# Hash attention and a SwiGLU block on one core: sums stored in two pieces, and x brought earlier, in the second block

## Chip, cores and metric

One core of one Trainium2 chip runs the whole program. The metric is the device time of an execution in microseconds (us). A kernel's time is the median of several executions.

## The reference

Attention with a hash mask, then a gated feed-forward block on its output:

```python
# q, k, v: (4, 8, 768, 64)   proj: (64, 6)
q_bucket = sum((q @ proj > 0) * 2**i);  k_bucket = sum((k @ proj > 0) * 2**i)
scores = where(q_bucket[:, None] == k_bucket[None, :], q @ k.T / 8, -1e9)
x = softmax(scores) @ v                  # all heads side by side: x is (3072, 512)
g = x @ w_gate                           # (512, 1536)
out = (g * sigmoid(g) * (x @ w_val)) @ w_out     # w_out: (1536, 512), out: (3072, 512)
```

## The kernel before

The program first does the attention (to 314 us of the span), and beside it and beside the first block splits the weights; then the feed-forward block in three blocks of 1024 rows of x. The stretch of this change is the second block and the start of the last one.

**Three parts for each number.** The matrix engine is fed with a rounded part, a rest and a difference of the two, in float32 form. So every operand is three arrays, made by three operations: `high` (ACT rounds), `low` (DVE takes the rest) and `diff` (DVE subtracts). Weights are split once and kept in DRAM tiles (`ram`); a ring of six tiles in on-chip memory is filled from there by `bring()`, whose loads GpSimd (POOL) issues in order.

**First and second block.** For each f of 12 there is a U: `one` (products of high and low, PE, tile `a`) for gate and value, then `other` (products of diff, tile `n`). ACT copies `a` into `n` (L849) before `other` may add to it, applies Silu (L862) for the gate, DVE multiplies (L872), and ACT and DVE split the result into `hid` (L881, L892, L895). A U is four steps, its slots 0 to 3; it takes 10.9 us of PE. After f = 3, 6, 9 and 11 there is a D, which multiplies three hids with `w_out`: eight chunks (slots 0 to 7), each with two ACT operations (L967, L923) and one of DVE (L973). So the order is U0 to U3, D 0, U4 to U6, D 1, U7 to U9, D 2, U10, U11, D 3.

**The last block** replaces 8 products of quarter matrices by 7, of sums of quarters of the weights and of x. Its sums are made in the second block, beside its products: for each p of 6 a gate and a value sum of weights (`("w", p, side)`), and four sums of x (`("x", j, side)`: xa, xb, ya, yb). `add` (L1090 to L1113, DVE) makes the sum in a tile `made`, of which there are two, one for each side (tags x2 and x3); `high` (L1119, ACT), `low` (L1125, L1127, DVE) and `diff` (L1134, L1138, DVE) split it; then the tile is stored to DRAM (`sums` and `xsums`, L1136 and L1140), by a DMA that SP issues. The next sum of the same side waits until that store has left the tile. The plan of slots is written out by hand with `put`: a step put at ("U", 4, 2) is recorded behind slot 2 of U4. Each engine runs its instructions in the order in which they were recorded, and each waits by semaphores for what it needs; SP's DMAs, too, are issued in the recorded order.

**What is brought for the last block.** x as the attention left it (`load_x`, L1050) goes into three tiles `words`; from its first quarter `first_quarter` makes B11 (L1199, L1203, L1207) into the tile x2, that a `made` had. `bring_sum` (L1188) loads the sums of x: T1 into x3, T2 and T3 into x0 and x1 when the second block's x has been used up; `fourth_sum` (L1216) loads T4 into the three `words` tiles.

**A group of the last block** is seven products, A11 to A22, one for each of the slots 1 to 6 that stand between them. Behind each, ACT and DVE take the result out (L1354, L1357, L1360) and free its bank. What remains of the group before, above all the split of its hid (`high`, `low`, `diff`: L1418, L1421, L1426), is recorded with `then(k, ...)` and runs at slot k of the next group.

Of the kernel before, what the change touches and what calls it, by code (L numbers as in the profile page):

```python
# [8 lines left out]
FP32 = mybir.dt.float32  # L9
# [10 lines left out]
def kernel(  # L20
# [771 lines left out]
    def gated_block(scope):  # L792
# [253 lines left out]
        def load_x(block, prs):  # L1046
            for pr in prs:
                t = wordp.tile([P, PIECE, 2], I32, tag="words", name="words")
                x = t.rearrange("p f w -> p (f w)").bitcast(FP32)
                nc.sync.dma_start(x, kept_x[pr][:, block * WB - S : (block + 1) * WB - S])  # L1050
                raw_x[block, pr] = x
# [70 lines left out]
        def low(key):  # L1122
            t = made[key]
            if key[0] == "w":
                tt(r32(t[:, :, 1]), t[:, :, 1], t[:, :, 0], op=ALU.subtract)  # L1125
            else:
                nc.vector.scalar_tensor_tensor(out=r32(t[:, :, 1]), in0=t[:, :, 0], scalar=-STEP,  # L1127
                                               in1=t[:, :, 1], op0=ALU.mult, op1=ALU.add)

        def diff(key):  # L1130
            t = made.pop(key)
            kind, n, side = key
            if kind == "w":
                nc.vector.scalar_tensor_tensor(out=r32(t[:, :, 2]), in0=t[:, :, 1], scalar=-STEP,  # L1134
                                               in1=t[:, :, 0], op0=ALU.mult, op1=ALU.add)
                nc.sync.dma_start(sums["gv"[side], n], t)  # L1136
            else:
                tt(r32(t[:, :, 2]), t[:, :, 0], t[:, :, 1], op=ALU.subtract)  # L1138
                for e in range(2):
                    nc.sync.dma_start(xsums[2 * side + e][:, n], t[:, e])  # L1140


        plan = {}
# [1 line left out]
        def put(kind, f, at, op, *args):  # L1145
            plan.setdefault((kind, f, at), []).append(lambda: op(*args))
# [23 lines left out]
                    put(*here, op, key)  # L1170
        put("U", 2, 0, load_x, LAST, (0, NP // 2))
        put("U", 4, 2, load_x, LAST, (1, 1 + NP // 2))
        xa, xb, ya, yb = (("x", j, side) for j in range(2) for side in range(2))
        for kind, f, at, op, key in (("U", 4, 0, add, xa), ("U", 4, 1, add, xb),
                                     ("U", 4, 2, high, xa), ("U", 5, 0, high, xb),
                                     ("U", 4, 3, low, xa), ("U", 4, 3, diff, xa),
                                     ("U", 5, 1, low, xb), ("U", 5, 1, diff, xb),
                                     ("D", 1, 3, add, ya), ("D", 1, 5, add, yb),
                                     ("D", 1, 5, high, ya), ("D", 1, 7, high, yb),
                                     ("D", 1, 6, low, ya), ("D", 1, 7, diff, ya),  # L1180
                                     ("U", 7, 0, low, yb), ("U", 7, 0, diff, yb)):
            put(kind, f, at, op, key)

# [2 lines left out]
        def bring_sum(i, pool, tag):  # L1186
            t = pool.tile([P, 2, 3, PIECE], FP32, tag=tag, name="xparts")
            nc.sync.dma_start(t, xsums[i])  # L1188
            xs[f"T{i + 1}"] = lambda v, j: t[:, j, v]

        def first_quarter():

            t = xparts_p.tile([P, 2, 3, PIECE], FP32, tag="x2", name="xparts")
            xs["B11"] = lambda v, j: t[:, j, v]
            x = [raw_x.pop((LAST, j))[:, 0:PIECE] for j in range(2)]

            def high():
                for j in range(2):
                    nc.scalar.activation(r32(t[:, j, 0]), x[j], AF.Copy, scale=TOWARD / STEP)  # L1199

            def low():
                for j in range(2):
                    nc.vector.scalar_tensor_tensor(out=r32(t[:, j, 1]), in0=t[:, j, 0], scalar=-STEP,  # L1203
                                                   in1=x[j], op0=ALU.mult, op1=ALU.add)

            def diff():
                nc.vector.tensor_tensor(r32(t[:, :, 2]), t[:, :, 0], t[:, :, 1], op=ALU.subtract)  # L1207

            return [high, low, diff]

        def fourth_sum():
            ts = []
            for v in range(3):
                t = wordp.tile([P, PIECE, 2], I32, tag="words", name="words")
                t = t.rearrange("p f w -> p (f w)").bitcast(FP32).rearrange("p (j c) -> p j c", j=2)
                nc.sync.dma_start(t, xsums[3][:, :, v])  # L1216
                ts.append(t)
            xs["T4"] = lambda v, j: ts[v][:, j]

        gens = {}  # L1220

# [6 lines left out]
        for i, (kind, n) in enumerate(order):  # L1228
            b, f = divmod(n, NF if kind == "U" else NF // NQ)
            if b == LAST - 1:  # L1230
                if kind == "U" and f == NF - 2:
                    assert not made
                    load_x(LAST, range(NP // 2))
                    splits.extend(first_quarter())
                elif kind == "U" and f == NF - 1:
                    bring_sum(0, xparts_p, "x3")
                    load_x(LAST, range(NP // 2, NP))
            elif (kind, f) == ("D", NF // NQ - 2):
                load_x(b + 1, range(NP // 2))
            elif kind == "U" and f >= NF - 2:  # L1240
                assert len(added) == NPIECE
                splits.extend(split_x(b + 1, f - NF + 2))
                if f == NF - 1:
                    load_x(b + 1, range(NP // 2, NP))
            if kind == "U":
                if b == LAST - 1 and f % 2 and f < NF - 1:
                    for side, what in enumerate("gv"):
                        ahead_of[what].append(lambda side=side: add(("w", f // 2, side), n))
            for at, atom in enumerate(gens.pop(i, None) or atoms_of(kind, n)):
                if kind == "U" and at == 2:  # L1250
                    sow_next(i)
                tail = atom()
                for entry in list(tails):
                    entry[0] -= 1
                    if not entry[0]:
                        tails.remove(entry)
                        entry[1]()
                if tail:
                    tails.append([1 if n % NF == NF - 1 else 2, tail])
                if kind == "U" and f >= NF - 2 and at and splits:  # L1260
                    splits.pop(0)()
                if kind == "D" and f == NF // NQ - 1:
                    if at == 0:
                        more = [split_x(b + 1, pr) for pr in range(NP // 2, NP)]
                        if b == LAST - 1:
                            for i_ in (1, 2):
                                bring_sum(i_, xparts_p, f"x{i_ - 1}")
                    if b == LAST - 1:
                        if at in (1, 2, 5, 7, 8, 9):
                            more[at in (2, 7, 9)].pop(0)()  # L1270
                        if at == 7:
                            fourth_sum()
                    elif at in (0, 7, 10):
                        for x in more:
                            x.pop(0)()
                count[0] += 1
                if left and count[0] in (4, 6, 11):
                    left.append(left.pop(0)())
                    left[:] = [f for f in left if f]
                    if count[0] == 4:  # L1280
                        bring(2)
                if kind == "U":
                    pace = (1, 2, 2, 2)
                elif n == 0:
                    pace = (0, 0, 0, 2, 1, 2, 2, 2)
                else:
                    pace = (0, 0, 1, 0) + (1,) * 8
                if b == LAST - 1:
                    for op in plan.pop((kind, f, at), ()):
                        op()  # L1290
                    continue
                if b == LAST - 2 and (kind, f) == ("D", NF // NQ - 1):
                    for op, key in opening.get(at, ()):
                        op(key)
                for _ in range(pace[at]):
                    step = next(mine, None)
                    if step:
                        step()
# [24 lines left out]
        def group(what, p):  # L1323
# [124 lines left out]
            then(2, lambda: low(0))  # L1448
            then(3, lambda: diff(0))
            then(3, lambda: high(1))  # L1450
            then(4, lambda: low(1))
            then(6, lambda: diff(1))

        gates = {}
# [48 lines left out]
```

## Time and profile before

| what | value |
|---|---|
| runs, us | 908.23, 905.15, 907.61 (median 907.61) |
| profiled execution, us | 906.43 |
| its span, us | 904.5 |
| PE busy | 892.4 us, 99% |
| DVE, ACT, POOL busy | 75%, 59%, 12% |
| second block | 510.8 to 717.4 us of the span |
| last block | from 717.4 us |

Times within the profile are counted from the start of the span; 1.9 us of the execution lie outside it. PE is matmul, ACT ScalarE, DVE VectorE, POOL GpSimd, SPq the sequencer of SyncE, which issues DMAs. A row of the timeline gives the start, the time to the end of the last instruction in it, the engine, the line of the kernel, the operation, what it writes and reads, and in brackets the idle time before it and who ended that. An idle engine that nobody waits for costs nothing.

### The profile page before, as it was taken

How to read it: one execution, taken by the hardware profiler on the slowest of the kernel's cores; microseconds unless marked ns; L12 is line 12 of the kernel's file. 1: busy time of each engine (PE TensorE's matmuls, PEld its weight loads, DVE VectorE, ACT ScalarE, POOL GpSimd, SP SyncE). 2: the span in 40 equal slices, each digit the busy share in tenths (PEclk: the TensorE clock that was granted, in tenths of full speed). 3: DMA queues.
4: the chain of work that ended last, by engine and by line, in shares of the span. 5: the costliest groups of instructions: out<-in, count | busy, mean ns of one | idle time of the engine just before them, and what ended most of it. 6: DMA issues, size and time to landing. Idle time of an engine off the chain costs nothing.

```text
span 904.5 us, 12799 instructions
## 1 busy us (share of the span) xinstructions
PE 892.4 (99%) x4731; PEld 624.3 (69%) x4731; DVE 678.8 (75%) x877; ACT 533.7 (59%) x782; POOL 107.0 (12%) x211
## 2 busy tenths in 40 slices
PE   9999999999999999999999999999998999999998
PEld 5444444444444488888888788867886877888887
DVE  6779999999988956649484978588682668377386
ACT  6788988788888645541423245355453667376470
POOL 2001100010001210101010010100010122121110
PEclk9999999999999999999999999999999999999999
DMA  7667778877787699776757787788869998297482
GB/s 180 111 147 183 188 205 193 211 214 217 226 196 214 218 355 355 265 268 213 278 192 278 287 324 299 297 303 327 312 235 377 374 355 284 102 331 265 158 278 93
DMA packets 149980, 224.06 MB, mean 248 GB/s; under 512 B 104000, under 2 KB 113696, under 8 KB 148000
## 3 DMA queue, kind: packets, MB, share of 16 engines
q0 software_dynamic: 25312, 128.99, 40.6%
q1 hardware_dynamic: 123200, 93.08, 34.3%
q10 hardware_dynamic: 1408, 1.20, 0.6%
q8 instruction: 37, 0.61, 0.3%
q14 instruction: 23, 0.19, 0.1%
HBM read 157.81 MB, written 64.59 MB: 246 GB/s over the span
## 4 chain that ended last, share of the span: by engine, by line
PE 74%; DVE 11%; issue 8%; DMA 5%; ACT 2%; POOL 1%; SPq 0%; POOLq 0%; DVEq 0%; ACTq 0%
PE sc L605 17%; PE av L636 14%; PE a L806 14%; PE o L806 13%; PE n L806 6%; PE y L806 3%; DMA sums_ram<-made 2%; PE joint L677 1%; DMA ring<-sums_ram 1%; DVE o L973 1%; PE joint L497 1%; PE x L806 1%; DVE hid L1421 1%; DVE hid L892 1%; DVE made L1125 1%
## 5 line engine op out<-in xcount | busy, mean ns | idle before, releaser
L806 PE MATMUL o<-ring,hid 128*128 128x512 f32 (+1 forms) x872 | 200.6, 389 | 2.3 <-DVE hid L892 1.0
L806 PEld LDWEIGHTS o<-ring,hid 128*128 128x128 f32 x872 | 162.4, 188 | 39.2 <-ACT o L923 2.1
L806 PE MATMUL a<-xparts,ring 128*128 128x512 f32 x768 | 178.1, 389 | 0.0
L806 PEld LDWEIGHTS a<-xparts,ring 128*128 128x128 f32 x768 | 144.1, 188 | 30.5 <-issue 0.6
L615 ACT ACTIVATE A<-sc 128x768 f32<-128x768 f32 x192 | 154.0, 814 | 1.6 <-PE sc L605 0.8
L605 PE MATMUL sc<-qT,kT 64*128 64x384 f32 x768 | 153.0, 483 | 0.0
L636 PE MATMUL av<-A,vraw 128*64 128x386 f32 (+1 forms) x768 | 127.7, 488 | 0.0
L849 ACT ACTIVATE n<-a 128x1024 f32<-128x1024 f32 x46 | 46.4, 1009 | 136.2 <-PE a L806 129.1
L308 POOL DMA_DIRECT2D ring<-ram x108 | 60.6, 563 | 389.7 <-PE n L806 119.1
L636 PEld LDWEIGHTS av<-A,vraw 128*64 128x64 f32 x768 | 53.7, 136 | 73.3 <-issue 62.4
L806 PE MATMUL n<-xparts,ring 128*128 128x512 f32 x384 | 93.3, 395 | 4.4 <-ACT n L849 4.4
L605 PEld LDWEIGHTS sc<-qT,kT 64*128 64x128 f32 x768 | 68.8, 187 | 39.8 <-issue 35.1
L806 PEld LDWEIGHTS n<-xparts,ring 128*128 128x128 f32 x384 | 72.9, 191 | 21.0 <-ACT n L849 5.8
L973 DVE TENSOR_TENSOR o<-o 128x512 f32<-128x512 f32 x84 | 56.9, 686 | 35.5 <-ACT o L967 20.1
L892 DVE SCALAR_TENSOR_TENSOR hid<-hid,v 128x1024 fp32r<-128x1024 f32 (+1 forms) x26 | 29.7, 1141 | 47.5 <-ACT hid L881 47.5
L967 ACT ACTIVATE o<-o 128x512 f32<-128x512 f32 x56 | 33.3, 596 | 53.5 <-PE o L806 52.5
L605 PE MATMUL sc<-qb,kb 64*128 64x384 bf16 x384 | 63.5, 323 | 0.0
L659 DVE SCALAR_TENSOR_TENSOR both<-A 128x1536 f32<-128x1536 f32 x32 | 55.5, 1733 | 3.9 <-ACT A L615 2.3
L663 DVE TENSOR_TENSOR both<-both,A 128x1536 f32<-128x1536 f32 x32 | 56.0, 1749 | 1.7
L806 PE MATMUL y<-xparts,ring 128*128 128x512 f32 x216 | 55.0, 390 | 0.0
L806 PEld LDWEIGHTS y<-xparts,ring 128*128 128x128 f32 x216 | 40.5, 188 | 8.9 <-DMA ring<-ram 0.5
L605 PEld LDWEIGHTS <-kb 64*128 64x128 bf16 x384 | 19.6, 94 | 32.5 <-issue 9.0
(219 smaller groups left out, 1074.8 us busy)
## 6 DMA issues: line engine op xcount, KB each, us to landing
ring<-ram POOLq DMA_DIRECT2D x96, 768.0 KB, 6.6
sums_ram<-made SPq DMA_DIRECT2D x12, 1536.0 KB
ring<-sums_ram POOLq DMA_DIRECT2D x24, 768.0 KB, 6.5
ram<-stage POOLq DMA_DIRECT2D x22, 768.0 KB, 4.3
ram<-stage SPq DMA_DIRECT2D x14, 768.0 KB
vraw<-in_v_dram SPq DMA_DIRECT2D x16, 384.0 KB
words<-xram SPq DMA_DIRECT2D x12, 512.0 KB
xsums<-made SPq DMA_DIRECT2D x8, 768.0 KB
```

The source lines that it names most:

```text
L308: nc.gpsimd.dma_start(t.bitcast(FP32)[:, :, cols], src[:, :, cols])
L497: nc.tensor.matmul(tile_[i * BLOCK : (i + 1) * BLOCK, 0:HQ], hash_w, T[name, n][:, half * HQ : (half + 1) * HQ], start=True, stop=True)
L605: nc.tensor.matmul(banks_of[u][:, h], x["k", n][rows, ks], x["q", n][rows, qs], start=start, stop=stop)
L615: nc.scalar.activation(weights(u)[:, :, 0:HQ], banks_of.pop(u), AF.Exp, scale=SCALE * (1.0 if units[u][0] else OFF / 2))
L636: nc.tensor.matmul(ps[h * D : (h + 1) * D, 0:width], raws["v", n][:, h, c, :], a[:, h, 0:width], start=c == 0, stop=c == NCH - 1)
L659: nc.vector.scalar_tensor_tensor(out=t, in0=first, scalar=S * EPS / P / 2, in1=now, op0=ALU.add, op1=ALU.add)
L663: nc.vector.tensor_tensor(t, t, now, op=ALU.add)
L806: nc.tensor.matmul(ps, w, x, start=start, stop=stop, **more)
L849: nc.scalar.activation(n_, a, AF.Copy, scale=-(STEP + 1))
L892: nc.vector.scalar_tensor_tensor(out=l_, in0=h_.bitcast(FP32), scalar=-STEP, in1=v_, op0=ALU.mult, op1=ALU.add)
L967: nc.scalar.activation(accs[c], t[:, 0], AF.Copy, scale=STEP + 1)
L973: nc.vector.tensor_tensor(accs[c], accs[c], t[:, 1], op=ALU.subtract)
```

## The change

Four edits. The sums are stored in two pieces: high and low right after `low`, and the difference after `diff`. x for the last block is loaded earlier: the first two of its four pieces are put at U8 and the third at U9 (before: U10, U11), the fourth stays at U11; the steps of `first_quarter` are put one slot later each than they ran, and its `bring_sum` at U10. T4 comes in three loads, put at slots 0, 5 and 7 of D 3, instead of all three at slot 7. The order of the operations for ya and yb in D 1 is another: ya's rounding is put one slot earlier, and ya's `low` ahead of yb's `add`. In the last block the `low` of the second hid runs at slot 6 instead of 4.

```diff
+            keep(key, slice(0, 2))          # at the end of low(key)
+
+        def keep(key, parts):
+            kind, n, side = key
+            t = made[key]
+            if kind == "w":
+                nc.sync.dma_start(sums["gv"[side], n][:, :, parts], t[:, :, parts])
+                return
+            for e in range(2):
+                nc.sync.dma_start(xsums[2 * side + e][:, n, parts], t[:, e, parts])
 
         def diff(key):
...
-                nc.sync.dma_start(sums["gv"[side], n], t)
...
-                for e in range(2):
-                    nc.sync.dma_start(xsums[2 * side + e][:, n], t[:, e])
+            keep(key, slice(2, 3))
+            made.pop(key)
...
+        put("U", 8, 0, load_x, LAST, range(NP // 2))
+        put("U", 9, 0, load_x, LAST, (NP // 2,))
...
-                                     ("D", 1, 3, add, ya), ("D", 1, 5, add, yb),
-                                     ("D", 1, 5, high, ya), ("D", 1, 7, high, yb),
-                                     ("D", 1, 6, low, ya), ("D", 1, 7, diff, ya),
+                                     ("D", 1, 3, add, ya), ("D", 1, 4, high, ya),
+                                     ("D", 1, 5, low, ya), ("D", 1, 5, add, yb),
+                                     ("D", 1, 6, diff, ya), ("D", 1, 7, high, yb),
                                      ("U", 7, 0, low, yb), ("U", 7, 0, diff, yb)):
...
+        fourth = []
+
         def fourth_sum():
-            for v in range(3):
-                ...
+            t = wordp.tile([P, PIECE, 2], I32, tag="words", name="words")
...
+            nc.sync.dma_start(t, xsums[3][:, :, len(fourth)])
+            fourth.append(t)
...
                 if kind == "U" and f == NF - 2:
-                    load_x(LAST, range(NP // 2))
-                    splits.extend(first_quarter())
-                elif kind == "U" and f == NF - 1:
-                    bring_sum(0, xparts_p, "x3")
-                    load_x(LAST, range(NP // 2, NP))
+                    steps = first_quarter()
+                    put("U", f, 1, bring_sum, 0, xparts_p, "x3")
+                    put("U", f, 2, steps[0])
+                    put("U", f, 3, steps[1])
+                    put("U", f + 1, 0, steps[2])
+                    put("U", f + 1, 0, load_x, LAST, (NP - 1,))
...
-                        if at == 7:
+                        if at in (0, 5, 7):
                             fourth_sum()
...
-            then(4, lambda: low(1))
+            then(6, lambda: low(1))
```

More of the change, by code (lines that the diff above doesn't have):

```diff
@@ L1128, in low @@
                                                in1=t[:, :, 1], op0=ALU.mult, op1=ALU.add)
+            keep(key, slice(0, 2))
[7 more added lines that the diff above has]
+                nc.sync.dma_start(xsums[2 * side + e][:, n, parts], t[:, e, parts])
         def diff(key):
-            t = made.pop(key)
-            kind, n, side = key
-            if kind == "w":
+            t = made[key]
+            if key[0] == "w":
                 nc.vector.scalar_tensor_tensor(out=r32(t[:, :, 2]), in0=t[:, :, 1], scalar=-STEP,
                                                in1=t[:, :, 0], op0=ALU.mult, op1=ALU.add)
-                nc.sync.dma_start(sums["gv"[side], n], t)
             else:
                 tt(r32(t[:, :, 2]), t[:, :, 0], t[:, :, 1], op=ALU.subtract)
-                for e in range(2):
-                    nc.sync.dma_start(xsums[2 * side + e][:, n], t[:, e])
+            keep(key, slice(2, 3))
+            made.pop(key)
         plan = {}
@@ L1209, in first_quarter @@
             return [high, low, diff]
+        fourth = []
         def fourth_sum():
-            ts = []
-            for v in range(3):
[L1214 to L1218, printed above, removed]
+            t = wordp.tile([P, PIECE, 2], I32, tag="words", name="words")
+            t = t.rearrange("p f w -> p (f w)").bitcast(FP32).rearrange("p (j c) -> p j c", j=2)
+            nc.sync.dma_start(t, xsums[3][:, :, len(fourth)])
+            fourth.append(t)
+        xs["T4"] = lambda v, j: fourth[v][:, j]
         gens = {}
```

## The prediction

> **What bounds the kernel now.** I read the page first: TensorE (PE) is busy 99% of the span, so only its idle and slowed time can be won.
>
> ```profile
> PE 892.4 (99%) x4731; PEld 624.3 (69%) x4731; DVE 678.8 (75%) x877; ACT 533.7 (59%) x782; POOL 107.0 (12%) x211
> ```
>
> Next, PE's timeline, where each row's start is set against an even pace. The undisturbed D at 656.65 to 672.97 has 72 matmuls in 16.32 us: 0.2267 us each. Every matmul here is of that shape.
>
> ```profile
> 603.83 0.39 PE L806 MATMUL n<-xparts,ring 128*128 128x512 f32 x1
> 604.51 1.20 PE L806 MATMUL o<-ring,hid 128*128 128x512 f32 x4 [0.29 <-ACT o L923]
> 605.92 0.50 PE L806 MATMUL o<-ring,hid 128*128 128x512 f32 x1 [0.21 <-DMA ring<-ram]
> 607.44 0.96 PE L806 MATMUL o<-ring,hid 128*128 128x512 f32 x3 [1.02 <-DVE hid L892]
> 608.70 10.72 PE L806 MATMUL o<-ring,hid 128*128 128x512 f32 x46 [0.30 <-DVE hid L895]
> ...
> 695.48 5.50 PE L806 MATMUL n<-xparts,ring 128*128 128x512 f32 x16 [4.21 <-ACT n L849]
> ```
>
> Four places lose time:
> - U10, U11 of the second block: 672.97 to 700.81 is 27.84 us for 96 matmuls; at pace 21.76. Loss 6.08: the stall, and 1.7 us because the 16 matmuls behind it ran slowly (5.33 us from 695.48 to 700.81, where the undisturbed row at 631.27 takes 3.62).
> - U6's second half and D 1: 600.23 to 624.01 is 23.78 us for 88; at pace 19.95. Loss 3.83.
> - First two groups of the last block: 717.43 to 737.82 is 20.39 us for 84; at pace 19.04. Loss 1.35.
> - Five y products that read "words" (745.98, 765.40, 806.97, 826.38, 867.63): rows of 1.88 or 1.90 where others take 1.52. Loss 5 x 0.36 = 1.8.
>
> Together 13.06. The timelines of ACT and DVE say who was late:
>
> ```profile
> 689.75 0.63 ACT L1199 ACTIVATE xparts<-words 128x512 fp32r<-128x512 f32 x1 [8.32 <-DMA words<-xram]
> 692.85 0.63 ACT L1199 ACTIVATE xparts<-words 128x512 fp32r<-128x512 f32 x1 [2.46 <-DMA words<-xram]
> 693.38 1.00 ACT L862 ACTIVATE g<-n 128x1024 f32<-128x1024 f32 x1
> 694.42 1.01 ACT L849 ACTIVATE n<-a 128x1024 f32<-128x1024 f32 x1
> ```
>
> PE needed the copy at 694.42 by 691.3; ACT stood in front of it, waiting for x. The second place:
>
> ```profile
> 586.00 0.69 DVE L1110 TENSOR_TENSOR made<-words 128x512 f32<-128x512 f32 x1 [8.39 <-DMA sums_ram<-made]
> ...
> 597.54 0.69 DVE L1090 TENSOR_TENSOR made<-ring 128x512 f32<-128x512 f32 x1 [0.48 <-DMA xsums<-made]
> ...
> 603.37 0.69 DVE L1090 TENSOR_TENSOR made<-ring 128x512 f32<-128x512 f32 x1 [2.42 <-DMA xsums<-made]
> ...
> 606.17 1.22 DVE L892 SCALAR_TENSOR_TENSOR hid<-hid,v 128x1024 fp32r<-128x1024 f32 x1
> ```
>
> A sum can't be begun before the store of the sum before it has left "made"; behind that wait stands L892, the hid that PE waits for at 607.44.
>
> **Part 1, x three f ahead.** Before, the queue of SP issues the two loads at 674.79, right behind the store at 674.42, and they land at 689.7 and 692.8, among 3 MB of stores and three ring loads (DMA share 0.99 from 673 to 683.9). After, in the built program's order, they stand behind the stores of x's last sum, so they go out near 632, in U7, sooner than the U8 of the edit, and the third near 653; the words tiles they take are free after add yb (before 626.4). The stores they now pass on SP's queue are not issued before 650, when 1 MB at some 400 GB/s (2.5 us) is long through. The rounding also moves from U10's slot 1 to slot 2, behind the Silu L862. It then waits only for the store of the g sum, which frees tile x2; in before that store was issued at 670.95, and the next sum's store needed at most 11.8 us (674.42 to the issue that waited for it, 686.63), so it is done by 682.8 at the worst, and ACT gets there near 683.2. Cover: 691.3 - 683.2 - 1.3 (two roundings) - 1.0 (the copy) = 5.8 us. I take 6.0 of 6.08; low end 4.4 (1.7 us of stall stays).
>
> Were a short stall to stay, the 1.7 us of slow matmuls would shrink with it by proportion to the row (4.21 us idle, 1.7 lost). The Trainium skill ("TensorE: Matmul & The Clock Gate", What's actually happening) has a threshold instead: the clock halves after an idle window of some 3.4 us. The clock of 0.91 in 680 to 700, and the full pace behind the 1.02 us wait at 607.44, agree with that; by it the whole 1.7 goes even if 2 us of stall stay, and this term would be 4.0 rather than 3.2 there.
>
> **Part 2, two pieces.** The first piece leaves after "low", one DVE operation of 1.14 us before "diff"; the last piece is a third of the bytes. xb's store before: issued 597.12 and 597.49 behind xa's, which went out at 592.34; it holds DVE to 603.37. After: the store that add xb waits for at 586.00 is cut the same way, so L1110, and behind it L872 and low and diff of xa, come 1 to 6 us earlier. xa's store is then through the queue before xb's first piece goes at about 595. 1.5 MB at the 393 to 418 GB/s of the DMA view is 3.7 us, with some 1 us to land: 599.7, 3.5 us earlier than 603.2. L892 then ends near 604 instead of 607.39, and L895 near 605, where PE, at pace, needs them at 605.1 and 605.8. Of 3.83 I take 3.3; ends 1.5 (the store only 1.5 us earlier) and 3.83. The tile's release also frees ring slots sooner (POOL's loads wait for L1090's reads), which covers the 0.21.
>
> What it adds: each weight sum is 256 packets of 4 KB and 256 of 2 KB instead of 128 of 12 KB. The trace's packet records give 159, 95 and 460 ns: (256 x 159 + 256 x 95 - 128 x 460) / 16 engines = 0.38 us; an x sum 0.32. For 12 and 4 sums 5.9 us of DMA time, against 28 us in which the DMA engines are idle between 540 and 680 (shares 0.88, 0.66, 0.87, 0.81, 0.90, 0.79, 0.66): nothing on the path, up to 0.8 (two sums) if the last pair's cover is gone. SP issues 24 more stores at 0.32 to 0.74 us; it waits over 100 us for L1134 in this stretch, so nothing. What is queued behind each on SP is the diff's own piece, then the next load; both wait for later DVE work anyway.
>
> The Trainium skill ("DMA: Bandwidth & Descriptors", Measured) speaks against it: batch to 1 MiB; 64 KB gets 138 GB/s and 1 MB 341. Read between these for a 0.5 MB piece, say 240, that would be an estimate of +0.7 us a sum, 11 us of DMA time in all, still within the idle time but not near the block's end. The packet rows decide; I keep 0.38.
>
> **Part 3, order in D 1.** High ya moves one chunk ahead, so ACT's L1119 now stands before L967 and the last L923. If add ya (1.4 us, then 1.05 on ACT) is late, the last chunk's matmuls wait. With DVE 3.5 us earlier it just fits: cost 0, end -1.2. low ya before add yb and diff later only lengthen what DVE does before U7, where it has gaps of 2.96 and 2.46.
>
> **Part 4, fourth sum in three loads, and less traffic.** The three loads (0.5 MB each) leave one by one in D 3 instead of at 713. Behind the second, which waits for L350 of x2 (709.73 + 1.14), stand output stores, and nobody needs their tiles before the next D at 768. From 700 to 740 the DMA share is 0.95 and 0.98, and the last block's second group waits for a ring load (0.69 at 729.50). 1.5 MB of x are gone from this stretch, but PE comes 6 us sooner. Of the 1.35 I take 0.4; ends -1.5 and +1.4.
>
> **Part 5, one rounding two products on.** L1421 at 745.26 (1.14 us) leaves the place before L1357 at 746.40, which frees y's bank; the DVE total up to the group's end is the same. All five 0.36 go. Two of them lie just ahead of a D, whose output weights arrive as PE asks (load issued 763.14, landed 768.23, PE waiting till 768.28); there the time is given back. I take 1.2; ends 0.9 and 1.8.
>
> Sum: 6.0 + 3.3 + 1.2 + 0.4 = 10.9, less 0.3 for parts 2 and 3: 10.6. The profiled execution took 906.43 (span 904.5); 906.43 - 10.6 = 895.8. The median of the runs is 1.2 above it; I put half of that on top: 896.4.
>
> **Rivals.** *DMA is the next bound*: 22.7 MB move between 680 and 740 at a ceiling of about 415 GB/s, 54.7 us in 60; less 1.5 MB 51.1 in 54. Room 3 us. If the first groups wait for rings and sums, 3.5 us come back, 899.9. For: shares 0.95 to 0.98; against: ring loads start when PE frees them, not at a fixed time.
>
> *Only a hand-over* (no change): ACT's rounding now waits for the g store instead of x, and in D 1 DVE for the last piece. If the first lands 8 us after 682.8 and the second when the whole store did, both losses stay and only the 1.2 of part 5 is won: 905.2. Against: the g store is issued first.
>
> *Slower*: the last piece lands later than the whole store did. A 0.5 MB DMA alone takes 2.26 us (out_dram at 889.99), so four more landings a pair, on a queue where the store at 674.42 took 11.8 behind ring loads, would delay L1090 and L872. It decides from some 3 us: at 4, D 1 loses 4 more, D 2 gets the same wait (4), the boundary still gains 2 and part 5 1.2: 906.4 + 4.8 = 911.2. Against: the same queue, and fewer bytes after diff.
>
> **How the numbers follow.** Forecast 0.70, DMA-bound 0.15, hand-over 0.07, slower 0.08. A measurement tells 0.3% (2.7 us) from no change; faster 0.70 + 0.15 = 0.85, plus 0.01 of the hand-over: 0.86; same 0.06; slower 0.08. The ends of the terms, all good, give 906.4 - 13.06 = 893.4; the DMA case with a low part 1 gives 902. Range 893 to 902.
>
> **What would show it.** Right: ACT's rounding near 680 without a wait on words; no PE wait for L849; L892 before 605 (less the shift) in D 1; y rows at 1.52. Wrong: L1090 or L1110 waiting longer for sums_ram or xsums, ACT's high waiting for sums_ram, PE waiting for ring or xparts after 711.

## The result, and the profile after

The changed kernel takes 904.17 us (median of 22 runs, 901.64 to 909.89), the kernel before 906.55 on the same chips (22 runs): ratio 0.9975, 95% interval 0.9964 to 0.9986. It is faster, by 2.4 us instead of the 10.2 forecast, and the time lies above the range. The profiled execution has a span of 901.4 us (before 904.5). The runs of the changed kernel scatter over 8.3 us, those of the kernel before over 3.3; a profile shows one of them. The five parts of the change are numbered below as in the prediction.

First PE's line of the page, then PE's timeline through the stretches that lost time before.

```profile
PE 890.9 (99%) x4731; PEld 624.9 (69%) x4731; DVE 678.7 (75%) x877; ACT 532.3 (59%) x782; POOL 106.8 (12%) x211
```

```profile
593.33 3.24 PE L806 MATMUL n<-xparts,ring 128*128 128x512 f32 x8 [1.84 <-ACT n L849]
...
607.80 12.63 PE L806 MATMUL o<-ring,hid 128*128 128x512 f32 x54
...
625.31 2.35 PE L806 MATMUL o<-ring,hid 128*128 128x512 f32 x9 [2.16 <-ACT o L923]
...
660.14 8.32 PE L806 MATMUL o<-ring,hid 128*128 128x512 f32 x36
669.29 8.48 PE L806 MATMUL o<-ring,hid 128*128 128x512 f32 x36 [0.82 <-ACT o L923]
677.60 7.42 PE L806 MATMUL a<-xparts,ring 128*128 128x512 f32 x32
...
695.74 3.79 PE L806 MATMUL n<-xparts,ring 128*128 128x512 f32 x16
699.36 17.22 PE L806 MATMUL o<-ring,hid 128*128 128x512 f32 x72
...
728.31 1.19 PE L806 MATMUL five__6030<-xparts,ring 128*128 128x512 f32 x4 [0.85 <-DMA ring<-sums_ram]
...
744.76 1.52 PE L806 MATMUL y<-words,ring 128*128 128x512 f32 x6
```

The boundary of U10 and U11 has no wait any more, and the product of 744.76, one of the five slow y rows, takes 1.52 instead of 1.88. But there are three waits that before did not have: in U5 (593.33), at the end of D 1 (625.31) and in D 2 (669.29). The starts of the same products in both traces give the account:

| stretch, by PE's rows | before, us | after, us | difference | forecast |
|---|---|---|---|---|
| D 0 to the start of D 1 (554.78 to 604.22; 555.06 to 607.80) | 49.44 | 52.74 | +3.30 | 0 |
| D 1 to the start of D 2 (to 656.65; to 660.14) | 52.43 | 52.34 | -0.09 | -3.3 (with U6) |
| D 2 (to 672.97; to 677.60) | 16.32 | 17.46 | +1.14 | 0 |
| U10, U11 (to 700.81; to 699.36) | 27.84 | 21.76 | -6.08 | -6.0 |
| D 3 and the first two groups (to 736.46; to 735.24) | 35.65 | 35.88 | +0.23 | -0.4 |
| the five y rows (to 877.54; to 874.72) | 141.08 | 139.48 | -1.60 | -1.2 |

With +0.28 ahead of D 0 and -0.28 behind the last row the sum is -3.10, the difference of the spans. (604.22 is the end of U6's last row in before.)

**The boundary.** ACT's timeline: the first quarter's rounding (L1210) follows the Silu without a wait, and L849 is back in its place at 685.06.

```profile
685.06 1.01 ACT L849 ACTIVATE n<-a 128x1024 f32<-128x1024 f32 x1 [2.62 <-PE a L806]
686.93 1.03 ACT L862 ACTIVATE g<-n 128x1024 f32<-128x1024 f32 x1 [0.86 <-PE n L806]
687.85 1.14 ACT L1210 ACTIVATE xparts<-words 128x512 fp32r<-128x512 f32 x2
```

**U5.** DVE's timeline, then ACT's. L1110, the first operation of add xb, begins at 588.30, not at 586.00 as before: it waits 11.56 us for the store of a weight sum, where it waited 8.39. ACT stands in L1119 (the rounding of xb; that of xa ran at 581.62), which needs add's last operation but is recorded ahead of U5's copy L849.

```profile
588.30 0.69 DVE L1110 TENSOR_TENSOR made<-words 128x512 f32<-128x512 f32 x1 [11.56 <-DMA sums_ram<-made]
...
604.36 0.69 DVE L1090 TENSOR_TENSOR made<-ring 128x512 f32<-128x512 f32 x1 [1.69 <-DMA xsums<-made]
...
607.16 1.22 DVE L892 SCALAR_TENSOR_TENSOR hid<-hid,v 128x1024 fp32r<-128x1024 f32 x1
```

```profile
591.08 1.06 ACT L1119 ACTIVATE made<-made 128x1024 fp32r<-128x1024 f32 x1 [3.92 <-DVE made L1113]
592.27 1.01 ACT L849 ACTIVATE n<-a 128x1024 f32<-128x1024 f32 x1
```

ACT's rows in before:

```profile
588.77 1.06 ACT L1119 ACTIVATE made<-made 128x1024 fp32r<-128x1024 f32 x1 [1.90 <-DVE made L1113]
589.97 1.01 ACT L849 ACTIVATE n<-a 128x1024 f32<-128x1024 f32 x1
```

There PE got the copy just in time; here a sum that came 2.3 us later became 1.84 us of idle PE. About as much again was lost to the clock: the 8 matmuls of 593.33 take 3.24 us, in experiment 3 below 2.11, and the 32 behind them 7.94, elsewhere 7.42. In the windows (columns: stretch, length, busy time of PE, PEld, DVE, ACT and POOL, granted clock, DMA share, GB/s) the clock is halved for 3.41 us:

```profile
590.58:593.99 3.41, 1.56 (x7) 0.98 (x7) 3.38 (x4) 2.78 (x3) 0.00 (x0) 1.00 0.50 151
593.99:597.40 3.41, 3.41 (x10) 2.63 (x9) 3.38 (x4) 1.17 (x2) 0.00 (x0) 0.50 0.96 379
```

So the question for the runs was why a store in two pieces lands later than the whole one. At that place, from 570 to 572 us, POOL issues three ring loads for U4, and SP the store (before 572.82; after 571.48 and 573.18). The packet records, counted from 579 to 583 us, show who gets the DMA engines:

| kernel | packet of the store | packets, store : ring load (6 KB each) |
|---|---|---|
| before | 12 KB | 94 : 82 |
| after | 4 KB (the first piece) | 174 : 157 |

The counts are about equal whatever the size (in single microseconds they scatter, from 20 : 23 to 30 : 19 in before). From equal counts, 12 KB packets would have two thirds of the bytes and 4 KB packets two fifths. The Trainium skill ("DMA: Bandwidth & Descriptors", Queues, rings and completion order) says that an engine goes round-robin between its queues, one whole packet at a time. The equal counts agree with taking turns, but the page's packet is a group of typically 9 to 17 descriptors, and no run here shows that a packet record is such a group. From this came the theory, called A below: *beside ring loads a store's share is set by its packet size*. The rival, C, was that what costs is the number of DMAs.

The records also show that the delay arises at the store's end. In the changed kernel only 11 of its packets are left at 585.00; from 585.6 on they go one every 0.31 us, the last at 587.48. A 2 KB packet takes 84 ns and a 6 KB one 234, so this looks like a DMA engine that is behind the others and still alternates with ring loads (the records do not name the engine). In before, two 12 KB packets are left at 584.1; they go 0.69 us apart (460 ns and 234), the last at 584.86.

### The profile page after: what moved, and what is told of

Same layout as the page of the kernel before. It is cut to its first block, busy times and chain, and to the rows that moved or that the text cites. A ratio compares the mean times of both kernels' runs of the same rounds, so it can differ in the third digit from the quotient of the medians.

```text
span 901.4 us, 12853 instructions
## 1 busy us (share of the span) xinstructions
PE 890.9 (99%) x4731; PEld 624.9 (69%) x4731; DVE 678.7 (75%) x877; ACT 532.3 (59%) x782; POOL 106.8 (12%) x211
## 4 chain that ended last, share of the span: by engine, by line
PE 78%; DVE 8%; DMA 7%; issue 6%; POOL 1%; ACT 0%; SPq 0%; POOLq 0%; DVEq 0%; ACTq 0%
PE sc L605 17%; PE av L636 14%; PE o L806 13%; PE a L806 13%; PE y L806 6%; PE n L806 6%; DMA sums_ram<-made 4%; PE x L806 2%; PE z L806 2%; PE joint L677 1%; DMA ring<-sums_ram 1%; PE joint L497 1%; DVE o L973 1%; DVE made L1144 1%; DVE made L1125 1%
## 5 line engine op out<-in xcount | busy, mean ns | idle before, releaser
L849 ACT ACTIVATE n<-a 128x1024 f32<-128x1024 f32 x46 | 46.4, 1008 | 143.4 <-PE a L806 134.7
L892 DVE SCALAR_TENSOR_TENSOR hid<-hid,v 128x1024 fp32r<-128x1024 f32 (+1 forms) x26 | 29.6, 1140 | 52.0 <-ACT hid L881 52.0
```

Of the source, the lines that this page charges most:

```text
L849: nc.scalar.activation(n_, a, AF.Copy, scale=-(STEP + 1))
L892: nc.vector.scalar_tensor_tensor(out=l_, in0=h_.bitcast(FP32), scalar=-STEP, in1=v_, op0=ALU.mult, op1=ALU.add)
```

## The experiments

The times are medians against the kernel before in the same runs; a ratio has its 95% interval in brackets. Edits are shown against the changed kernel where nothing else is said.

**1. Every sum stored whole again** (the other parts of the change kept).

```diff
-            keep(key, slice(0, 2))          # at the end of low(key)
...
-            keep(key, slice(2, 3))
+            keep(key, slice(0, 3))
```

> The changed kernel with every sum stored whole again, behind diff (part 2 undone; the rest of the change stays). Theory A (packet share): beside ring loads the DMA engines alternate packet by packet, so a store in packets of 4 KB beside ring packets of 6 KB gets less of the rate than one in packets of 12 KB. Then DVE's wait of add xb ends near 586 again (588.3 in the changed kernel, 586.0 before), U5's stall of 2.2 us and the slow matmuls behind it go (3.6 us), the entry of D 1 waits for hid as before (about 2.9), D 1's last chunks wait 1 us or less, D 2 not at all. Net about 899 to 901 us by the measure where before is 906.5. Theory B (the loads put ahead or the new order delay that store, its pieces do not matter): 588 stays, the stall in U5 stays, 903 to 905.

Measured: 901.15 us, 0.9935 (0.9923 to 0.9947): 3.0 us less than the changed kernel. DVE's row is back where it was, and so is ACT's; U5 has no wait.

```profile
586.20 0.69 DVE L1110 TENSOR_TENSOR made<-words 128x512 f32<-128x512 f32 x1 [7.77 <-DMA sums_ram<-made]
```

So the two pieces, which were to win 3.3 us, cost 3.0 beside the other parts. What remains lost in D 1's entry and end is not theirs.

**2. Weight sums in two DMAs by rows** (12 KB packets, 64 rows each), meant to part the number of DMAs from the packets' size.

```diff
+                for r in (slice(0, P // 2), slice(P // 2, P)):
+                    nc.sync.dma_start(sums["gv"[side], n][r], t[r])
```

> As e1, but each weight sum is stored behind diff by two DMAs of 64 rows each, in packets of 12 KB: twice the number of DMAs, large packets. Theory A: as e1, add xb near 586, no stall in U5 beyond 0.3 us, same time as e1 within 1 us. Theory C (the number of DMAs delays the landing: a fixed time for each, one more semaphore to wait for): add xb at 588 or later, U5 stall of 2 us and the slow clock behind it, 3 us slower than e1.

Measured: 919.85 us, 1.0137 (1.0115 to 1.016). It told nothing about the question, for it brought a cost of its own: alone on the DMA engines (576 to 580 us) the store from 64 rows moved 197 GB/s, its packets took about 1.0 us instead of 0.46, and L1110 came at 593.51.

```profile
593.51 0.69 DVE L1110 TENSOR_TENSOR made<-words 128x512 f32<-128x512 f32 x1 [6.13 <-DMA sums_ram<-made]
```

**3. The old order in D 1** (ya's rounding and low back where they were), two pieces kept.

```diff
-  ("D", 1, 3, add, ya), ("D", 1, 4, high, ya), ("D", 1, 5, low, ya), ("D", 1, 5, add, yb), ("D", 1, 6, diff, ya),
+  ("D", 1, 3, add, ya), ("D", 1, 5, add, yb), ("D", 1, 5, high, ya), ("D", 1, 6, low, ya), ("D", 1, 7, diff, ya),
```

> The changed kernel with the order of ya and yb in D 1 as before (part 3 undone). Theory D: the wait of 2.3 us at 622.75 in D 1 is ACT's L1119 for ya, now in front of the last L923, waiting for add ya; without it that stall is under 0.6 us. U5 stays as in the changed kernel. About 901.5 to 902.5 us. Rival: DVE is late in D 1 whatever the order, and the last chunk waits as long: 904.

Measured: 902.46 us, 0.9946 (0.9928 to 0.9964). The wait of 2.16 us at D 1's end is gone; U5's is there still.

```profile
594.12 2.11 PE L806 MATMUL n<-xparts,ring 128*128 128x512 f32 x8 [2.36 <-ACT n L849]
...
621.61 4.39 PE L806 MATMUL o<-ring,hid 128*128 128x512 f32 x18 [0.38 <-ACT o L923]
```

The 1.7 us between the medians are not the price of the order alone, for other waits differ too: D 1's entry waits 0.56 us for a hid here and not in the changed kernel, and the clock stayed at full speed behind U5's wait:

```profile
589.52:592.94 3.42, 2.24 (x10) 1.51 (x9) 3.35 (x6) 1.06 (x1) 0.00 (x0) 1.00 0.56 162
592.94:596.35 3.41, 2.23 (x10) 1.85 (x11) 3.38 (x4) 2.89 (x3) 0.00 (x0) 1.00 0.52 209
```

Experiment 7 gives the price of the order more cleanly.

**4. The two pieces alone, on the kernel before.**

> The kernel before with the stores in two pieces and nothing else. Theory A: U5 stalls 2 us and its matmuls behind run slowly (3.6 us lost), the entry of D 1 no longer waits for hid (2.9 won) because PE comes later, the stall of 4.4 us in U11 stays: 906 to 908, no gain. Theory of the prediction (the store leaves the tile sooner): 3 us faster than before, 903.5.

Measured: 907.47 us, 1.0007 (0.9988 to 1.0027): not told from no change. L1110 comes at 587.72, and PE waits in U5 without any other part of the change. At the boundary the wait is half of what it was (ACT waits 6.17 us for x instead of 8.32):

```profile
592.76 2.11 PE L806 MATMUL n<-xparts,ring 128*128 128x512 f32 x8 [2.00 <-ACT n L849]
...
693.86 5.52 PE L806 MATMUL n<-xparts,ring 128*128 128x512 f32 x16 [2.12 <-ACT n L849]
```

By its rows the profiled execution loses 2.2 us in U5 and wins 2.1 at the boundary and 1.3 at D 1; but it is among the quicker of twelve runs (904.74, of 903.37 with a mean clock of 1.000 to 913.00 with 0.994), and over all of them nothing is won. With x loaded ahead there is nothing left for the pieces to win at the boundary.

**5. One whole store of 2 KB packets.** On experiment 1; the weight sums' DRAM tiles are spaced, so that the one DMA can't join its pieces. Number of DMAs as in before, packets a sixth.

```diff
-  dram.tile([P, 2, 3, PIECE], ...)
+  dram.tile([P, 2, 3, PIECE + P], ...)[:, :, :, 0:PIECE]
```

> e1 (each weight sum stored whole by one DMA behind diff), with the tiles of the weight sums in DRAM spaced out so that the one DMA goes in packets of 2 KB instead of 12 KB (the ring's loads of these sums too, which is a cost in the last block). Theory A (alternating packet by packet, so the store's share of the rate is its packet size against the ring's 6 KB): from 578 on the store gets 2 of 8 parts of some 415 GB/s, about 104 GB/s, while ring loads are queued (to about 588); add xb begins at 589.5 or later (e1: 586.2), and U5 stalls 3 us or more. Theory C (it is the number of DMAs, or their fixed times): one DMA as in e1, add xb at 586.2, no stall in U5.

Measured: 906.73 us, 1.0001 (0.9991 to 1.001), 5.6 us more than experiment 1. The count from 578 to 582 us is 206 : 189, L1110 waits longest of all, and PE 4.68 us:

```profile
590.34 0.69 DVE L1110 TENSOR_TENSOR made<-words 128x512 f32<-128x512 f32 x1 [12.64 <-DMA sums_ram<-made]
```

```profile
595.38 3.45 PE L806 MATMUL n<-xparts,ring 128*128 128x512 f32 x8 [4.68 <-ACT n L849]
```

Theory C falls: this is one DMA. The end of the store is drawn out most here, one 2 KB packet every 0.31 us from 585.9 to 589.68. In the profiles U5 alone loses 6.5 us against experiment 1. The last block, whose loads of these sums go in smaller packets too, loses 1.5 more, and other stretches are shorter by about as much. The spaced tiles are a second difference, but they did not slow the packets: 2 KB take 84 to 86 ns here and 84 in the changed kernel.

**6. The same with 6 KB packets**: the space stands behind all three parts together instead of behind each.

> As the run with 2 KB, but spaced so that the one DMA goes in packets of 6 KB, and the ring's loads stay as they are. Theory A: half the rate beside the ring, 208 GB/s: 1.57 MB in 7.6 us instead of 5.7; add xb begins between 586.2 and 588.3, near 587.3, U5 stalls about 1 us, the time is e1's plus 0.5 to 2 us. Theory C: as e1.

Measured: 902.23 us, 0.9954 (0.9937 to 0.997), count 145 : 126 from 579 to 583 us, L1110 (here one line further down) at 586.64, a wait of 0.95 in U5.

```profile
586.64 0.69 DVE L1111 TENSOR_TENSOR made<-words 128x512 f32<-128x512 f32 x1 [8.50 <-DMA sums_ram<-made]
```

With whole stores the idle time before this row goes 7.77, 8.50 and 12.64 us for packets of 12, 6 and 2 KB, and the time 901.15, 902.23 and 906.73. That is theory A's order; the step from 12 to 6 KB is small (in time the intervals overlap, in U5 it is the wait of 0.95), the one to 2 KB large.

**7. Whole stores and the old order** (experiments 1 and 3 together).

> e1 with the order of ya and yb in D 1 as before: parts 2 and 3 undone, the loads ahead, T4 in three loads and part 5 stay. Theory D: e1's wait of 1.2 us at 621.45 goes, the rest is as in e1: 899.5 to 900.5 us. Rival (D 1 is short of DVE whatever the order): as e1, 901.

Measured: 899.01 us, 0.9918 (0.9903 to 0.9933). Against experiment 1 the old order alone is worth 2.1 us by the medians; in the two profiles U6's second half and D 1 take 1.3 less.

**8. Pieces for the x sums only**, on experiment 7.

```diff
+            if key[0] == "x":
+                keep(key, slice(0, 2))          # in low(key)
...
-            keep(key, slice(0, 3))
+            keep(key, slice(2 if key[0] == "x" else 0, 3))
```

> As e5, but the sums of x in two pieces as in the changed kernel; the weight sums stay whole. If the pieces cost time only where ring loads stand beside them, the x pieces (593 to 604, no ring load) win: L892 in D 1 comes 1 us earlier than in e5, about 1 us of the entry of D 1: 898.5 to 899.5. If pieces cost everywhere: slower than e5.

Measured: 898.29 us, 0.9909 (0.9894 to 0.9923). The wait that part 2 was meant for is halved, from 1.82 to 0.90, and PE's wait for hid L892 (0.48 in experiment 7) is gone. These are DVE's rows in experiment 7 and here:

```profile
602.34 0.69 DVE L1090 TENSOR_TENSOR made<-ring 128x512 f32<-128x512 f32 x1 [1.82 <-DMA xsums<-made]
```

```profile
601.77 0.69 DVE L1090 TENSOR_TENSOR made<-ring 128x512 f32<-128x512 f32 x1 [0.90 <-DMA xsums<-made]
```

The medians differ by 0.7 us, the intervals overlap: the wait is shown, the gain of time is not firmly.

**9. Part 1 alone, on the kernel before.**

> The kernel before plus part 1 alone: x's loads at U8 and U9, the first quarter's steps one slot later. Sums stored whole behind diff, old order in D 1, low at slot 4, fourth sum as before. If part 1 is worth what the boundary lost (6.1) and has no price, the time is 906.6 - 6.1 = 900.5, D 2 keeps its even pace, and y's five rows and the loss at D 1's entry (3.8) stay. If the loads ahead are what makes D 2 stall (0.6 to 1.2 in every run that has them), a step of about 1 us over pace is there in D 2 and the time is 901.5 or so. If the stall in D 2 belongs to the later PE of the other runs, D 2 is free of it here too.

Measured: 901.68 us, 0.9945 (0.9932 to 0.9957). The boundary has its whole 6.08 us back. D 2 keeps its pace (16.32 us, from 656.74), so loads ahead do not by themselves make it wait. But not all of the gain reaches the time. U6's second half and D 1 (599.40 to 624.10) take 0.9 us more than in before, with the clock at 0.50 from 608.00 to 611.42. D 3 and the first two groups (694.82 to 731.38) take another 0.9 more: PE reaches the second group of the last block sooner, and there it waits twice for the ring.

```profile
722.12 1.65 PE L806 MATMUL y<-xparts,ring 128*128 128x512 f32 x6 [0.60 <-DMA ring<-ram]
724.41 1.21 PE L806 MATMUL five__6010<-xparts,ring 128*128 128x512 f32 x4 [0.64 <-DMA ring<-sums_ram]
```

**10. Experiment 8 with x's loads later**, behind the stores of U9.

```diff
-        put("U", 8, 0, load_x, LAST, range(NP // 2))
-        put("U", 9, 0, load_x, LAST, (NP // 2,))
+        put("U", 9, 1, load_x, LAST, range(NP // 2))
+        put("D", 2, 0, load_x, LAST, (NP // 2,))
```

> The best version so far (weight sums whole, x sums in two pieces, old order in D 1; 298 matters less than the difference: it ran at 898.3) with x's first two loads at slot 1 of U9 and the third at slot 0 of D 2, so that they go out behind the stores that U7 and U9 wait for. If D 2's stall of 0.8 comes from x's loads sharing the DMA engines with ring loads and stores ahead of D 2, it goes or shrinks, and the time is 897.5. If the stall comes only from DVE's own order, it stays and the time is 898.3. If the loads now meet D 2's own ring loads and the last weight sum's stores, the first quarter's rounding in U10 waits for them: a stall of 1 us or more at the boundary and 900 or above.

Measured: 897.46 us, 0.9899 (0.9884 to 0.9915), the lowest of all (its interval overlaps that of experiment 8): it beats both kernels, the one before by 1%. D 2 has its even pace, and the boundary still no wait.

```profile
655.47 16.48 PE L806 MATMUL o<-ring,hid 128*128 128x512 f32 x72
```

About D 2: in the changed kernel DVE's add there waits for the two weight sums' stores (0.72 and 0.38 us), and ACT's L923 behind it:

```profile
661.92 0.69 DVE L1090 TENSOR_TENSOR made<-ring 128x512 f32<-128x512 f32 x1 [0.72 <-DMA sums_ram<-made]
...
665.72 0.69 DVE L1090 TENSOR_TENSOR made<-ring 128x512 f32<-128x512 f32 x1 [0.38 <-DMA sums_ram<-made]
```

```profile
668.63 0.60 ACT L923 ACTIVATE o<-o 128x512 f32<-128x512 f32 x1 [1.20 <-DVE o L973]
```

In the eleven profiled executions that stand for comparison (all but experiment 2) D 2 loses its pace exactly where one of these two rows waits for its store: not in before and in experiments 4, 9 and 10, but in all others. By the issues, two things come together there. The last ring load for U9 is still under way for more than 2 us after the first of these stores goes out (to 658.05 against 652.09 in the changed kernel, 652.83 against 649.32 in experiment 8; in before, 9 and 10 only for 1.6 to 1.7 us), and x's third load follows right behind the second store (in experiment 4 it does not). Experiment 10 puts the first two loads of x behind these stores, so that they no longer stand beside the ring loads, and D 2's loss went. That both things are needed is read from the traces only, not tried one by one.

## Why the prediction was wrong

Three of the runs lie between the two kernels and make a chain of steps that adds up to the time, by medians: before 906.5; part 1 alone 901.7 (-4.8); parts 4 and 5 added 899.0 (-2.7); the new order in D 1 added 901.2 (+2.1); the pieces added 904.2 (+3.0). A step's size holds beside the steps ahead of it: alone, on the kernel before, the pieces are not told from no change (experiment 4).

- **Part 1, x ahead** (6.0): right in size and mechanism, 6.08 at the boundary in the changed kernel and in experiment 9. ACT got to the rounding at 687.85, later than the 683.2 of the working, because PE was 4.6 us later there. That only 4.8 of it reach the time in experiment 9 is told there.
- **Part 2, the pieces** (3.3): this step failed. The text: "the store that add xb waits for at 586.00 is cut the same way, so L1110, and behind it L872 and low and diff of xa, come 1 to 6 us earlier". L1110 came 2.3 us later. What was wrong is the sum for the pieces: packets of 159 and 95 ns were counted by their own length (0.38 us a sum) and set against idle DMA time averaged over 140 us. The store is in a race with three ring loads just when it goes out, and there smaller packets yield a smaller share: experiments 1, 5 and 6 show it. Most of the packets are gone almost as early as in before; the few at the end, which still take turns with 6 KB ring packets, make the delay. The rival "the last piece lands later than the whole store did" named the mechanism, with a price of 4 us from 3 us of delay on; it came with 2.3, because ACT's copy for U5 had almost no slack (2.3 us later, it let PE idle 1.84 us). The place that it named, D 1 and D 2, was wrong: U5 was.
- **The clock.** The forecast charged no slow matmuls behind short waits. Here 1.84 us of idle PE were followed by a halved clock, and in experiment 4 2.12 us, while 2.36 us in experiment 3 left it at 1.00. The prediction's own rule (loss in proportion to the wait) and the threshold that it set beside it both miss this. The clock record of the twelve profiled executions shows what decides. The clock is 1.00 or 0.50, and between 10 and 880 us each of the seven halvings lasts 3.41 us and begins a whole multiple of 3.41 us after the clock's last change. So there is a grid of windows, and against the program it lies differently in each execution. With 0.2267 us for each matmul from its start, the windows just before a halving hold at most 1.29 us of matmuls, and every window before full clock at least 1.48. In the changed kernel the wait fell into one window (590.58 to 593.99, 1.29 us); in experiment 3 the longer one was cut by a border at 592.94 (2.08 and 2.10). The Trainium skill ("TensorE: Matmul & The Clock Gate", What's actually happening) names an idle window of some 3.4 us that runs free; the traces agree with its length and with the free running, but a window need not be wholly idle. So a wait of 2 us can cost up to another 1.7 (half of 3.41) or nothing, by where it falls.
- **Part 3, the order in D 1** ("just fits: cost 0, end -1.2"): mis-sized: it cost 2.1 from experiment 7 to 1 by the medians, 1.3 in D 1 by the profiles. Its premise, DVE 3.5 us earlier, did not come. The timelines of the changed kernel, DVE's and then ACT's, show how: ya's sum waits for a weight sum's store, and L1119, now recorded ahead of the last L923, waits 2.49 us for that sum.

```profile
621.77 0.69 DVE L1107 TENSOR_TENSOR made<-words 128x512 f32<-128x512 f32 x1 [1.08 <-DMA sums_ram<-made]
```

```profile
623.22 1.06 ACT L1119 ACTIVATE made<-made 128x1024 fp32r<-128x1024 f32 x1 [2.49 <-DVE made L1108]
...
624.66 0.59 ACT L923 ACTIVATE o<-o 128x512 f32<-128x512 f32 x1
```

- **D 2** was costed at nothing and lost 1.14; the cause is read from the traces (experiment 10). The prediction let x's loads go out in U7 and U9 and only asked whether they land in time, not what they share the DMA engines with.
- **Part 4** (0.4): against before the stretch took 0.23 more, against experiment 9 it took 0.7 less in experiment 7. The rival "DMA is the next bound" is seen in small, in the 0.9 that experiment 9 gives back in D 3 and the first groups.
- **Part 5** (1.2): right, all five y rows at 1.52, 1.6 us. Between experiments 9 and 7 the medians differ by 2.7, against 1.6 forecast for parts 4 and 5; by the profiles' rows 2.3 of that lie in their stretches. Of the rest, D 1, where experiment 9 had the halved clock, is 1.4 shorter and D 2 0.7 longer.

## What to carry to other kernels

A store that is cut for an earlier start also gets smaller packets, and beside another queue's loads a smaller share of the DMA engines: look at what is queued at the moment it goes out, not at the average share, and cut it, if at all, where nothing else is moving (here the x sums, which cost nothing in pieces and may have won 0.7, not the weight sums). When an engine runs its list in order, look for the operation with the least slack behind each wait that moves: here a copy that had been just in time for PE. A short wait of PE can cost half a window of the clock on top. And a part that is right on its own can be eaten by two others, so try the parts singly; the best version here keeps only some of the change's parts.

## What was not expected of the hardware

- Two queues share the DMA engines by packets, not by bytes: 94 : 82, 145 : 126, 174 : 157 and 206 : 189 packets in 4 us against the ring loads' 6 KB, for packets of 12, 6, 4 and 2 KB.
- A store can land late by a few packets: the last of 2 KB went one every 0.31 us, up to 587.48 in the changed kernel and 589.68 in experiment 5, when nearly all the others were gone by 585.
- A store that takes only 64 of the 128 rows moves 197 GB/s alone on the engines, where stores and loads together reach some 430.
- The granted clock halves for 3.41 us behind a window of 3.41 us in which PE had at most 1.29 us of matmuls, and did not behind 1.48 us or more; the windows lay on a grid that stood differently against the program in each execution. So a wait of 1.84 us was followed by a halved clock and one of 2.36 us was not.
